# A new order for all operations of a gated recurrence with a highway layer behind it

## The chip, the cores and the metric

The kernel runs on one core of a Trainium2 chip. The metric is the time of one execution on the device, in microseconds; the lower the better. A core has five engines that work side by side, each on its own list of instructions, in order: TensorE (PE, matrix products; its weight loads are shown as PEld), VectorE (DVE), ScalarE (ACT), GpSimd (POOL) and SyncE (SP), which here issues nearly all transfers. They wait for each other by semaphores.

## The reference

There are two parts, one behind the other. For each of 4 sequences of 6336 tokens with 256 channels, a gate is made from f_logit, and a recurrence runs along the tokens:

```
sig = 1.0 / (1.0 + np.exp(-f_logit))
f = lower_bound[None, None, :] + (1.0 - lower_bound[None, None, :]) * sig
i = 1.0 - f
for t in range(S):
    h = f[:, t] * h + i[:, t] * x[:, t]
    y[:, t] = h
```

Then each token's row y goes through a highway layer:

```
H = np.maximum(y @ w_h, 0.0)
T = 1.0 / (1.0 + np.exp(-(y @ w_t + b_t)))
return T * H + (1.0 - T) * y
```

Inputs and output are float32; 25344 tokens are read twice (x and f_logit) and written once.

## The kernel before

The 25344 tokens are cut into 29 units (line 42): two of 256 tokens, three of 512, 22 of 1024, one of 512 and one of 256. The 256 channels are two halves of 128. Each unit goes through the same operations, and each operation has a letter. In a name such as f0.1 the first number is the unit and the second the half (or the piece):

- l, x: SP loads f_logit and x of the unit (line 256), tokens on the partitions.
- u: ACT makes 1 - sigmoid(f_logit), in 16 bit (line 268).
- b: the product u*x of one half (line 276), on POOL, or on DVE where the name has a v.
- i: PE transposes u of one half, 128 tokens at a time (line 284), so that channels lie on the partitions.
- f: the gate from the transposed u and the lower bound, on ACT (line 295) or, with a v, on DVE (line 293).
- p: PE transposes the products b (line 304).
- s: DVE's scan along the tokens (line 323), which is the recurrence. It begins with the last value of the unit before, of the same half, except at the start of a sequence. Its result y stands without the factor 1 - lower_bound; that factor is in the weights and in a diagonal matrix.
- z, g: PE multiplies y by the two weights (lines 335 and 115).
- t: ACT's sigmoid of z (line 348). d: DVE's max of g and y, from which y is subtracted through the weights (line 352). Line 212 takes the identity off w_h for that.
- e: the product d*t (line 358), on POOL, or on DVE with a v; a unit has one, two or three of them.
- o: PE adds y (times the diagonal, line 380) and d*t (line 381) and turns the tokens back onto the partitions. c: the copy of that into SBUF, on ACT (line 393) or, with a v, on DVE (line 391). w: SP stores it (line 397).

Operations without numbers come once: pc and pb transpose the lower bound and the bias on PE (line 194), cc makes ncc and cc of the lower bound on DVE (lines 200 and 201), cb copies the bias, dg makes the diagonal, wh and wt load the two weights, IW takes the identity off on POOL, WHa and WTa scale and shorten the weights on ACT (line 228). k*N allocates a place in PSUM and runs N matmuls on zeros (lines 126 and 115) whose results nobody reads; the three matmuls of line 154 are of that kind too.

All of this is one list, written by hand into the program as a string of names (line 49 on). The loop at line 399 goes through it, calls the function of each letter, and pins the instructions, so that each engine runs its operations in the order of the list. The number behind a colon is the slot: the buffer in SBUF, or the part of PSUM, that the result uses. An operation that reuses a slot waits until the earlier content has been read. So the list settles three things: the order on each engine, the engine of b, f, e and c, and the buffer of each result. SP's transfers are in the list too: SP issues them in order, and a store that waits for its copy holds up the loads behind it.

DVE and POOL share a port to SBUF in this program's reckoning: behind a product or scaling on DVE that the list marks, the next POOL product waits for it (line 178). Nothing makes DVE wait for POOL in the same way.

Of the kernel before, what the change touches and what calls it, by code (L numbers as in the profile page):

```python
# [19 lines left out]
def kernel(  # L20
# [37 lines left out]
b6.0:5 f6.1:2 d4.0 k*3:1 p6.1:0 s6.1:4 i6.0:1 l8:2 u7:3 z5.1:1 g5.1:2 x8:2 b7.1:6 b7.0:7 f6.0:0 t4.0 t5.1:2 i7.1:1 p6.0:0
z5.0:0 f7.1:1 d5.1:2 t5.0 o3.0:1 g5.0:2 i7.0:1 c3.0:3 s6.0:5 e5.1v w1.0 l9:3 e4.0 x9:3 w0.0 e5.2v p7.1:0 l10:4 w2.0 d5.0 e5.0
g6.0:0 z6.1:1 z6.0:2 u8:0 f7.0:3 t6.1:1 i8.0:1 e4.1v b8.0:1 b8.1:0 s7.1:6 f8.0v:2 l11:5 w3.0 t6.0 x10:4 x11:5 u9:1 d6.0:0  # L60
i8.1:0 g6.1:1 p7.0:1 s7.0:7 o5.1:2 f8.1:0 c5.1:1 o5.0:0 i9.1:0 d6.1 e6.0 p8.1:1 c5.0:0 f9.1:1 e6.2 z7.0:2 t7.0:0 o4.0:0
p8.0:0 c4.0:2 u10:2 w5.1 b9.1:3 e6.1 l12:0 w4.0 l13:1 g7.1:1 s8.1:2 i9.0:1 g7.0:2 o6.0:0 s8.0:3 i10.1:0 f9.0:3 b9.0:2 x12:0
p9.1:1 u11:3 b10.0:4 b10.1:5 b11.0:6 d7.1:2 d7.0 e7.0 z8.1:1 g8.1:2 s9.1:0 f10.1:0 p9.0:0 t8.1:2 c6.0:3 d8.1:1 i11.1:1 s9.0:1
o6.1:1 z7.1:0 f11.1:2 c6.1:1 i10.0:1 t7.1 g8.0:2 p10.0:0 z9.0:1 w6.0 w5.0 f10.0v:1 d8.0 u12:0 t9.0:1 z9.1:0 w6.1 e8.1v e7.2v
t9.1 e7.1v l14:2 x13:1 i12.1:1 f12.1:3 z8.0:2 g9.0:1 o7.1:0 s10.0:4 b11.1:7 t8.0 i11.0:1 p10.1:0 l16:3 f11.0:1 o7.0:2 u13:1
c7.0:2 d9.0:0 l15:4 e8.0 e8.2 g9.1:1 p11.0:1 s10.1:5 i13.1:0 s11.0:6 c7.1:3 f13.1:0 b12.1:0 o8.0:2 d9.1 o8.1:0 p11.1:1
i13.0:0 z10.0:1 b12.0:1 e9.0 c8.0:0 g10.0:2 s11.1:7 d10.0:2 c8.1:1 g10.1:0 f13.0:1 t10.0:0 w7.0 u14:2 w7.1 p12.1:0 z10.1:1
d10.1 z11.0:2 g11.1:0 t10.1 s12.1:2 i12.0:1 d11.1:1 t11.0:2 f12.0:2 x14:2 w8.0 w8.1 b13.1:3 z11.1:1 p12.0:0 o9.1:2 e10.0
t11.1 x15:3 l18:5 u15:3 s12.0:3 g11.0:0 p13.1:1 o9.0:1 d11.0 i14.1:0 b13.0:2 z12.0:0 c9.1:2 s13.1:0 f14.1:3 c9.0:3 o10.1:2
e11.0v x16:4 i15.1:0 p13.0:1 t12.0:1 o10.0:1 c10.1:0 f15.1:2 s13.0:1 b14.0:4 b14.1:5 c10.0:1 g12.1:0 g12.0:2 i14.0:0 w9.1  # L70
w9.0 d12.1:0 i15.0:1 d12.0 l17:0 g13.0:1 g13.1:0 z12.1:2 u16:0 f15.0:0 f14.0:1 d13.0:2 p14.0:1 b15.0:6 b15.1:7 d13.1 t12.1
w10.1 s14.0:4 w10.0 e12.0 o11.1:1 z13.0:0 u18:1 p14.1:0 o11.0:2 s14.1:5 b16.0:0 t13.0:0 x17:5 i18.0:1 l19:1 c11.1:2 w11.1
c11.0v:3 z13.1:0 f18.0:1 t13.1 g14.0:1 d14.0:1 i16.0:0 w11.0 b16.1:1 e13.0 p15.0:1 l20:2 f16.0:3 u17:2 z14.0:2 s15.0:6
o12.0:0 g14.1:1 i16.1:0 t14.0:2 b17.0:3 c12.0:0 x18:0 p15.1:1 o12.1:2 d14.1 s15.1:7 f16.1:0 w12.0 z14.1:1 c12.1:1 p16.0:0
i17.0:1 t14.1 g15.1:0 z15.0:2 w12.1 x19:1 s16.0:2 p16.1:0 f17.0:2 o13.0:1 d15.1:0 u19:3 t15.0:1 p17.0:1 o13.1:0 c13.0:2
c13.1:3 b17.1:2 e14.0 s16.1:3 z15.1:2 i17.1:0 g16.0:1 s17.0:0 g16.1:0 d16.0:2 t15.1 f17.1:3 x20:2 d16.1 u20:0 i18.1:1 z16.0:2
t16.0:0 p17.1:0 g15.0:1 z16.1:0 f18.1:0 w13.1 l21:4 b18.0:4 b18.1:5 t16.1 s17.1:1 w13.0 o14.0:2 d15.0 l22:3 i19.1:1 o14.1:0
# [12 lines left out]
e23.1 p25.0:0 c22.0:1 s25.0:0 f25.1:1 e23.2v z24.0:1 z24.1:0 g24.1:2 i26.1:0 p25.1:1 t24.0:0 f26.1:3 t24.1 d24.1:2 s25.1:1  # L90
z23.0:1 g24.0:2 w21.1 l27:3 i26.0:0 b26.0:4 b26.1:5 t23.0 o22.1:0 z25.1:1 p26.1:1 d24.0 e24.2v x27:3 u27:0 w22.0 w20.1 x28:4
g25.0:2 c22.1:3 e24.0 t25.1:1 b27.1:6 e24.1 e23.0v b27.0:7 b28.0:0 f26.0:1 s26.1:4 d25.0:0 w22.1 o23.1:0 z25.0:1 c23.1:1
p26.0:0 i27.1:1 o23.0:0 f27.1:3 t25.0 c23.0:0 g25.1:2 w21.0 s26.0:5 i27.0:1 f27.0:1 o24.1:1 p27.0:0 o24.0:0 p28.0:1 c24.1:3
# [344 lines left out]
```

## Time and profile before

| what | value |
|---|---|
| median of 3 runs | 206.66 us (206.52 to 207.08) |
| profiled execution, first to last instruction | 204.7 us |
| median of the runs less that span | 1.96 us |
| busy: DVE, ACT, PE, POOL | 193.0, 193.1, 191.6, 175.6 us |
| DMA, mean rate | 384 GB/s, 78.68 MB |

The profile gives one execution, and its span is that execution's own time from the first instruction to the last. What a run takes before and after it is in the 1.96 us. Busy time is the time in which an engine had an instruction in work; it does not say whether another engine waited for it. So the busy times are read by stretches of the span. In rows of groups, the columns are line, engine, operation, what is written and read, shape, count; then the busy time and the mean in ns; then the idle time of the engine just before, and what ended it.

### The profile page before, as it was taken

The page shows a single profiled execution, that of the slowest core. Times are in us where ns is not written, and L with a number is a line of the kernel's source. Part 1 is how long each engine was busy: PE and PEld are TensorE (multiplying, and loading weights), DVE is VectorE, ACT ScalarE, POOL GpSimd, SP SyncE. Part 2 cuts the span into 40 slices and gives each one's busy share as a digit, 9 for nine tenths or more (in the row PEclk, how much of TensorE's full clock was granted, in tenths as well). Part 3 has the DMA queues.
Part 4 walks back from the last instruction along what each step waited for, and adds up shares of the span by engine and source line. Part 5 has one row for each costly group of instructions (what it writes and reads, how often), then busy time and mean ns, then how long its engine had stood idle before and what let it go on. Part 6 is the DMA issues. An engine that isn't in the chain of part 4 may idle for free. (4 is left out here: it accounts for less than half of the span.)

```text
span 204.7 us, 4658 instructions
## 1 busy us (share of the span) xinstructions
PE 191.6 (94%) x1826; PEld 131.9 (64%) x1826; DVE 193.0 (94%) x162; ACT 193.1 (94%) x201; POOL 175.6 (86%) x98
## 2 busy tenths in 40 slices
PE   7889999989899899999999999999998999999990
PEld 2455656576567757757666577776776677677680
DVE  2799999999999999999999999999999999999990
ACT  4799999999999999999999999999999999999771
POOL 3146699899996999799999979999979999989960
PEclk9999999999999999999999999999999999999998
DMA  5999999999999999999999999999999998970986
GB/s 176 387 415 429 410 421 415 413 424 420 422 419 411 429 423 415 425 415 422 428 402 426 429 417 419 418 425 423 413 337 400 425 390 307 352 283 22 396 330 241
DMA packets 16413, 78.68 MB, mean 384 GB/s; under 512 B 1796, under 2 KB 2568, under 8 KB 10760
## 3 DMA queue, kind: packets, MB, share of 16 engines
q1 hardware_dynamic: 16384, 78.39, 94.7%
q8 instruction: 14, 0.23, 0.4%
q14 instruction: 7, 0.06, 0.1%
q10 hardware_dynamic: 8, 0.00, 0.0%
HBM read 52.43 MB, written 25.95 MB: 383 GB/s over the span
## 5 line engine op out<-in xcount | busy, mean ns | idle before, releaser
L276 POOL TENSOR_TENSOR bv<-u,x 128x1024 bf16<-128x1024 f16 (+2 forms) x53 | 104.2, 1988 | 14.8 <-DVE d L358 5.7
L323 DVE TENSOR_TENSOR_SCAN y<-f,y,bT 128x1024 bf16<-128x1024 f16 (+5 forms) x56 | 106.9, 1925 | 0.2
L358 POOL TENSOR_TENSOR d<-d,t 128x512 bf16<-128x512 bf16 (+3 forms) x32 | 70.4, 2213 | 4.1 <-DVE d L358 1.8
L352 DVE SCALAR_TENSOR_TENSOR d<-y,ncc,g 128x1024 bf16<-128x1024 bf16 (+2 forms) x58 | 63.2, 1105 | 0.3 <-PE g L115 0.2
L348 ACT ACTIVATE t<-z,bt 128x1024 bf16<-128x1024 f32 (+2 forms) x58 | 62.4, 1112 | 0.8 <-PE z L115 0.8
L295 ACT ACTIVATE f<-uT,ncc 128x1024 f16<-128x1024 f16 (+2 forms) x55 | 60.8, 1120 | 0.8 <-DVE y L323 0.2
L393 ACT COPY o<-op 128x1024 f32<-128x1024 f32 (+2 forms) x53 | 52.8, 1036 | 1.9 <-ACT t L348 1.0
L268 ACT ACTIVATE u<-l 128x2048 f16<-128x2048 f32 (+2 forms) x29 | 51.5, 1776 | 2.5 <-DMA l<-in_f_logit_dram 2.5
L380 PE MATMUL op<-diag,y 128*128 128x128 f16 x396 | 49.7, 219 | 0.9 <-ACT t L348 0.4
L381 PE MATMUL op<-ident_b,d 128*128 128x128 bf16 x396 | 49.7, 219 | 0.8 <-POOL d L358 0.8
L381 PEld LDWEIGHTS <-d 128*128 128x128 bf16 x396 | 44.0, 113 | 4.8 <-POOL d L358 1.7
L380 PEld LDWEIGHTS <-y 128*128 128x128 bf16 x396 | 44.2, 113 | 2.3
L335 PE MATMUL z<-y,w_sb 128*128 128x512 bf16 (+1 forms) x116 | 40.0, 368 | 0.8 <-DVE d L352 0.3
L335 PE MATMUL g<-y,w_sb 128*128 128x512 bf16 (+1 forms) x116 | 40.3, 368 | 0.0
L304 PE MATMUL bT<-ident_f,bv 128*128 128x128 f32 x198 | 32.1, 278 | 2.9 <-DVE y L323 1.1
L115 PE MATMUL g<-y,w_sb 128*128 128x512 bf16 x88 | 33.3, 379 | 0.0
L115 PE MATMUL z<-y,w_sb 128*128 128x512 bf16 x88 | 33.3, 379 | 0.0
L284 PE MATMUL uT<-ident_h,u 128*128 128x128 f16 x396 | 31.4, 219 | 2.0 <-DVE y L323 1.1
L284 PEld LDWEIGHTS <-u 128*128 128x128 f16 x396 | 25.9, 98 | 11.1 <-issue 3.1
L335 PEld LDWEIGHTS <-w_sb 128*128 128x128 f16 x232 | 22.3, 98 | 15.7 <-ACT f L295 0.2
L304 PEld LDWEIGHTS bT<-ident_f,bv 128*128 128x128 f32 x198 | 22.1, 140 | 13.3 <-issue 4.7
L115 PEld LDWEIGHTS <-w_sb 128*128 128x128 f16 x176 | 17.2, 98 | 15.8 <-issue 1.7
(35 smaller groups left out, 53.6 us busy)
## 6 DMA issues: line engine op xcount, KB each, us to landing
out_dram<-o SPq DMA_DIRECT2D x48, 512.0 KB, 9.7
l<-in_f_logit_dram SPq DMA_DIRECT2D x22, 1024.0 KB, 14.0
x<-in_x_dram SPq DMA_DIRECT2D x22, 1024.0 KB, 14.3
l<-in_f_logit_dram SPq DMA_DIRECT2D x4, 512.0 KB, 6.3
x<-in_x_dram SPq DMA_DIRECT2D x4, 512.0 KB, 7.6
x<-in_x_dram SPq DMA_DIRECT2D x3, 256.0 KB, 3.7
l<-in_f_logit_dram SPq DMA_DIRECT2D x3, 256.0 KB, 4.3
out_dram<-o SPq DMA_DIRECT2D x2, 256.0 KB, 14.8
```

Of the source, the lines that this page charges most:

```text
L115: return pe.add_instruction(mybir.InstMatmult(name=nc.get_next_instruction_name(), start_tensor_calc=start, stop_tensor_calc=stop, tile_si ...
L276: shared(pin(e.tensor_mul(bv[:, :nb // 2].rearrange("p k d j -> p k j d"), st[n]["u"][:, :nb, own].rearrange("p (k j) d -> p k j d", j=2), ...
L284: pin(nc.tensor.transpose(uT[:, j * P:(j + 1) * P], st[n]["u"][:, j, h * P:(h + 1) * P], ident_h))
L295: pin(nc.scalar.activation(to, of, AF.Identity, scale=ncc[:, h:h + 1], bias=1.0))
L304: pin(nc.tensor.transpose(words[:, k:k + g * (P - 1) + 1:g], pair, ident_f))
L323: pin(nc.vector.tensor_tensor_scan(y[:, c:e], st[n]["f", h][:, c:e], st[n]["bT", h][:, c:e], 0.0 if fresh else carry[h], op0=ALU.mult, op1 ...
L335: pin(nc.tensor.matmul(p[:, a:e], w, half(n, "y", ki)[:, a:e], start=ki == 0, stop=ki == NH - 1))
L348: pin(nc.scalar.activation(half(n, "t", m), st[n]["z", m][:, :tokens(n)], AF.Sigmoid, bias=bt[:, m:m + 1]))
L352: pin(nc.vector.scalar_tensor_tensor(half(n, "d", m), half(n, "y", m), ncc[:, m:m + 1], st[n]["g", m][:, :tokens(n)], op0=ALU.mult, op1=AL ...
L358: shared(pin(e.tensor_mul(st[n]["d"][:, a:c], st[n]["d"][:, a:c], st[n]["t"][:, a:c])), not eng)
L380: pin(nc.tensor.matmul(o, half(n, "y", h)[:, cols], diag[:, h], start=True, stop=False))
L381: pin(nc.tensor.matmul(o, half(n, "d", h)[:, cols], ident_b, start=False, stop=True))
```

## The change

The string is replaced by another one. The functions, the cut into units, the number of buffers and what is computed stay. The first lines of the diff show how it reads:

```
-k*3:a0 x0:0 pc:0 l0:0 l1:1 cc u0:0 k*3:1 pb:2 i0.0:1 k*4:0 dg wh u1:1 b0.1v:0 f0.0:0 b0.0v:1 i1.0:0 x1:1 l2:2 wt IW f1.0v:1 p0.0:1
...
+l0:0 k*1:a0 x0:0 u0:0 b0.0:0 i0.0:1 pc:0 cc i0.1:0 l1:1 f0.0:0 p0.0:1 f0.1v:1 x1:1 k*3:1 k*1:2 wh b0.1v:1 wt IW u1:1 s0.0:0 p0.1:0
...
```

Both hold the same 850 names, apart from the v. The new string is three lines shorter, so lines behind it have numbers that are 3 lower: DVE's gate at line 293 is line 290 there.

Operations that change engines:

| | to DVE | away from DVE |
|---|---|---|
| f (ACT or DVE) | f0.1, f1.1 (256 tokens), f2.0, f3.1 (512) | f8.0, f10.0 (1024) |
| b (POOL or DVE) | none | b0.0 (256) |
| e (POOL or DVE) | e5.0, e6.0, e24.0, e25.0 (1024 columns), e6.2, e24.1, e25.2, e27.0, e27.1 (512), e10.0, e13.0, e14.0, e20.0 (2048), e28.0, e28.1 (256) | e0.0, e0.1, e1.0, e1.1 (256), e3.1, e4.1, e5.2, e7.1, e7.2, e8.1, e23.2, e24.2 (512), e23.0 (1024), e11.0, e16.0, e19.0 (2048) |
| c (ACT or DVE) | c6.1, c8.0 (1024), c26.0 (512) | c26.1, c26.2 (512) |

The matmuls on zeros in the string go from 27 to 16. Transfers: the list of SP begins with x0 l0 l1 wh x1 l2 wt before, and with l0 x0 l1 x1 wh wt l2 now. Later l4 stands ahead of x3, l8 ahead of x7, and x19 stands behind x21, l22 and w13.0.

At three places the order of an engine is shown, before and now. The first is DVE's beginning; 128x256 is a half of unit 0 or 1, and y<-f,bT is the scan. Before:

```order
L200 TENSOR_SCALAR ncc<-lbT 128x2
L201 TENSOR_SCALAR cc<-lbT 128x2
L217 TENSOR_SCALAR diag<-ident_h,cc 128x128 x2
L276 TENSOR_TENSOR bv<-u,x 128x2x128 x2
L293 TENSOR_SCALAR f<-uT,ncc 128x256
L207 COPY bt<-tbT 128x2
L323 SCALAR_TENSOR_TENSOR y<-f,bT 128x256
L276 TENSOR_TENSOR bv<-u,x 128x2x128 x2
```

And now:

```order
L197 TENSOR_SCALAR ncc<-lbT 128x2
L198 TENSOR_SCALAR cc<-lbT 128x2
L290 TENSOR_SCALAR f<-uT,ncc 128x256
L273 TENSOR_TENSOR bv<-u,x 128x2x128
L320 SCALAR_TENSOR_TENSOR y<-f,bT 128x256
L273 TENSOR_TENSOR bv<-u,x 128x2x128
L214 TENSOR_SCALAR diag<-ident_h,cc 128x128 x2
L320 SCALAR_TENSOR_TENSOR y<-f,bT 128x256
L290 TENSOR_SCALAR f<-uT,ncc 128x256
```

The first gate and the first scan stand further ahead, one product b has gone to POOL, and the diagonal comes behind the first scan.

The second place is PE's beginning, where lbT is what DVE's ncc is made of. Before:

```order
L115 LDWEIGHTS zeros
L115 MATMUL idle<-zeros 128x512
L194 MATMUL lbT<-ident_f,lb 128x2
L126 LDWEIGHTS zeros
L126 MATMUL idle<-zeros 128x512
L115 LDWEIGHTS zeros
L115 MATMUL idle<-zeros 128x512
L115 LDWEIGHTS zeros
L115 MATMUL idle<-zeros 128x512
L194 MATMUL tbT<-ident_f,tb 128x2
L284 LDWEIGHTS u
L284 MATMUL uT<-ident_h,u 128x128
```

And now:

```order
L123 MATMUL idle<-zeros 128x512
L281 LDWEIGHTS u
L281 MATMUL uT<-ident_h,u 128x128
L281 LDWEIGHTS u
L281 MATMUL uT<-ident_h,u 128x128
L191 MATMUL lbT<-ident_f,lb 128x2
L281 LDWEIGHTS u
L281 MATMUL uT<-ident_h,u 128x128
```

The lower bound's transpose has gone behind the first two transposes of u0, and the matmuls on zeros ahead of it are four where there were six.

The third place is DVE's end, with the units 26 to 28. Before:

```order
L352 SCALAR_TENSOR_TENSOR d<-y,ncc,g 128x512
L391 COPY o<-op 128x512
L352 SCALAR_TENSOR_TENSOR d<-y,ncc,g 128x256
L391 COPY o<-op 128x512
L352 SCALAR_TENSOR_TENSOR d<-y,ncc,g 128x256
L391 COPY o<-op 128x512
```

And now:

```order
L355 TENSOR_TENSOR d<-d,t 128x512
L388 COPY o<-op 128x512
L349 SCALAR_TENSOR_TENSOR d<-y,ncc,g 128x256
L388 COPY o<-op 128x512
L349 SCALAR_TENSOR_TENSOR d<-y,ncc,g 128x256
L355 TENSOR_TENSOR d<-d,t 128x256 x2
```

The two products of unit 28, which POOL made, stand at DVE's end, behind the last d; the third copy is ACT's.

More of the change, by code (lines that the diff above doesn't have):

```diff
@@ L58 @@
[L58 to L77, printed above, removed]
@@ new lines @@
+z5.1:0 e4.1 s6.0:4 e4.0 i7.0:1 d5.1:2 p6.1:0 b7.1:6 t5.1:2 s6.1:5 z5.0:1 f7.0:1 i7.1:1 g5.0:0 u8:0 o3.0:2 f7.1:3 d5.0 p7.1:0 s7.1:6
+b7.0:7 i8.0:1 b8.0:1 t5.0 g6.0:0 z6.0:1 f8.0:2 c3.0:3 w0.0 w2.0 u9:1 p7.0:1 d6.0:0 x9:3 i8.1:0 l10:4 s7.0:7 e5.2 z6.1:2 g6.1:0 t6.1:0
+o4.0:2 f8.1:0 b8.1:0 t6.0 c4.0:4 d6.1 i9.1:1 p8.0:0 e5.0v z7.1:0 z7.0:1 l12:5 g7.0:2 e6.2v e5.1v f9.1:3 i9.0:1 e6.0v s8.0:0 d7.0:1
+t7.1:1 g7.1:0 u10:2 t7.0 e6.1 f9.0:1 p8.1:0 o6.0:2 d7.1 c6.0:0 o6.1:1 i10.0:1 o5.0:0 l11:0 w1.0 b9.1:2 s8.1:1 f10.0:2 b9.0:3 x10:4
@@ new lines @@
+c5.0:2 g8.0:2 c6.1v:1 x11:5 i10.1:0 u11:3 p9.1:1 g8.1:1 e7.2 d8.0:0 e7.0 b10.0:4 z8.0:0 s9.1:4 f10.1:0 z8.1:2 p9.0:0 d8.1 w4.0 i11.1:1
+b10.1:5 w3.0 x12:0 l13:1 t8.0:2 s9.0:5 w6.0 w6.1 b11.1:6 t8.1 f11.1:3 o7.1:0 o5.1:1 l15:2 k*0:2 p10.1:1 c7.1:4 u12:0 z9.1:2 x13:1
+b11.0:7 g9.1:0 t9.1:0 s10.1:2 p10.0:0 c5.1:3 i12.0:1 z9.0:2 d9.1:2 f12.0:1 s10.0:3 e7.1 g9.0:0 w5.0 i11.0:1 o7.0:1 d9.0 t9.0 p11.0:0
+l14:3 z10.1:2 f11.0:0 u13:1 p11.1:1 g10.1:0 e8.2 e8.0 b12.0:1 e8.1 x14:2 c7.0:0 t10.1:1 s11.0:6 s11.1:7 i13.1:0 o8.1:1 o8.0:2 i12.1:1
@@ L99 @@
+o27.1:0 z28.1:a0 c27.0:3 w26.1 z28.0:a1 d28.1:1 g28.0:1 c27.1v w26.0 t28.1:1 d28.0 e28.1v w27.0 t28.0 e28.0v o28.0:2 c28.0:1 o28.1:a0
+c28.1:4 w28.0 w28.1
 """
```

63 lines of the change are left out of this document (35 added, 28 removed).

## The prediction

> **What bounds the kernel now.** I read the page first (span, busy time, slices), then the busy time by stretch, then the groups by shape, then the order of time at both ends. The page:
>
> ```profile
> span 204.7 us, 4658 instructions
> PE 191.6 (94%) x1826; PEld 131.9 (64%) x1826; DVE 193.0 (94%) x162; ACT 193.1 (94%) x201; POOL 175.6 (86%) x98
> DVE  2799999999999999999999999999999999999990
> ACT  4799999999999999999999999999999999999771
> ```
>
> Four engines stand at 86 to 94%, so the average tells nothing. The slices do: DVE is short of full only in the first two slices and the last. By stretch (length; busy time of PE, its weight loads, DVE, ACT and POOL, each with its count of instructions; granted clock; share of the DMA engines; GB/s):
>
> ```profile
> 20.00:180.00 160.00, 154.56 (x1507) 108.58 (x1508) 159.68 (x113) 160.00 (x150) 150.12 (x66) 1.00 1.01 409
> 180.00:190.00 10.00, 10.00 (x106) 7.49 (x106) 9.83 (x9) 8.91 (x10) 9.53 (x8) 1.00 0.39 155
> 190.00:200.00 10.00, 9.69 (x115) 7.40 (x113) 9.13 (x14) 8.00 (x14) 7.69 (x7) 1.00 0.92 361
> ```
>
> For 160 us DVE is idle for 0.32 us and ACT for none; POOL has 9.9 us to spare. DVE stays at 91 to 98% to the end, while ACT falls to 80%. The DMA engines are full too, but the waits (total, times, longest) show what the transfers cost the engines:
>
> ```profile
> ACT u L268 <- DMA l<-in_f_logit_dram: 2.5, 2, 1.3
> POOL bv L276 <- DMA x<-in_x_dram: 0.2, 1, 0.2
> ```
>
> That is 2.7 us in all, and the 2.5 fall on the first two loads. So the bound is DVE's own work, with ACT close behind; a charge on late transfers mends something that hardly costs here. The question is what the new table does to DVE's work and to the little time DVE is idle.
>
> **DVE's work.** The table also hands operations to other engines. Rows by shape (count, then busy and mean ns):
>
> ```profile
> L358 DVE TENSOR_TENSOR d<-d,t 128x2048 bf16<-128x2048 bf16 x4 | 5.3, 1354 | 0.0
> L358 DVE TENSOR_TENSOR d<-d,t 128x512 bf16<-128x512 bf16 x13 | 5.1, 424 | 0.1
> L358 DVE TENSOR_TENSOR d<-d,t 128x256 bf16<-128x256 bf16 x4 | 0.9, 282 | 0.0
> L358 DVE TENSOR_TENSOR d<-d,t 128x1024 bf16<-128x1024 bf16 x1 | 0.7, 678 | 0.0
> L293 DVE TENSOR_SCALAR f<-uT,ncc 128x1024 f16<-128x1024 f16 x2 | 2.5, 1258 | 0.0
> L293 DVE TENSOR_SCALAR f<-uT,ncc 128x256 f16<-128x256 f16 x1 | 0.5, 483 | 1.4 <-PE uT L284 1.4
> L391 DVE COPY o<-op 128x1024 f32<-128x1024 f32 x1 | 1.2, 1199 | 0.0
> L391 DVE COPY o<-op 128x512 f32<-128x512 f32 x3 | 2.1, 691 | 0.4 <-PE op L381 0.2
> L276 DVE TENSOR_TENSOR bv<-u,x 128x256 bf16<-128x256 f16 x4 | 1.5, 434 | 0.0
> L323 DVE TENSOR_TENSOR_SCAN y<-f,y,bT 128x256 bf16<-128x256 f16 x4 | 2.7, 720 | 0.0
> ```
>
> The tables give the counts (the last row, a scan, is for the head). Gained: f of 256, two (0.97); f of 512, two; product d·t of 1024, three (2.03), of 2048, one (1.35); copy of 1024, two (2.40). No row has f of 512 on DVE: each lies between 0.48 and 1.26, and the straight line between those rows gives 0.74, so 1.48 for two. Sum 8.23. Lost: f of 1024, two (2.52); d·t of 512, three (1.27), of 256, two (0.56); b of 256, one (0.43); copy of 512, one (0.69). Sum 5.47. Net +2.76, and +2.24 to +3.80 by the ends of f. Two corrections. Neighbours overlap a little:
>
> ```profile
> 98.43 1.20 DVE L391 COPY o<-op 128x1024 f32<-128x1024 f32 x1
> 99.54 1.27 DVE L352 SCALAR_TENSOR_TENSOR d<-y,ncc,g 128x1024 bf16<-128x1024 bf16 x1
> ```
>
> The copy's 1.20 would end at 99.63, and the next begins at 99.54; with one instruction more in all that is -0.1. And the mean of 1354 ns holds one product that was held up (below); a free one takes 1.20: -0.15. I take **+2.5**. The scans and the 58 d stay as they are.
>
> ACT goes the other way:
>
> ```profile
> L295 ACT ACTIVATE f<-uT,ncc 128x1024 f16<-128x1024 f16 x42 | 53.0, 1278 | 0.0
> L295 ACT ACTIVATE f<-uT,ncc 128x512 f16<-128x512 f16 x8 | 5.4, 687 | 0.8 <-DVE y L323 0.2 <-PE uT L284 0.2
> L295 ACT ACTIVATE f<-uT,ncc 128x256 f16<-128x256 f16 x5 | 2.4, 491 | 0.0
> L393 ACT COPY o<-op 128x1024 f32<-128x1024 f32 x42 | 47.1, 1163 | 0.0
> L393 ACT COPY o<-op 128x512 f32<-128x512 f32 x9 | 5.1, 588 | 1.8 <-ACT t L348 1.0 <-PE op L381 0.8
> ```
>
> Two f of 1024 more (2.56) and one copy of 512 (0.59), less two f of 512 (1.37), two of 256 (0.98) and two copies of 1024 (2.33): **-1.5**. POOL is lighter by more, PE by 11 dummy matmuls. In 20 to 180 us these cannot be paid to DVE: it has 0.32 us to win there. Nothing covers the +2.5.
>
> **The head.** In order of time:
>
> ```profile
> 2.87 1.06 PE L115 MATMUL idle<-zeros 128*128 128x512 bf16 x2
> 4.14 0.63 ACT L268 ACTIVATE u<-l 128x512 f16<-128x512 f32 x1 [1.29 <-DMA l<-in_f_logit_dram]
> 4.16 0.16 DVE L200 TENSOR_SCALAR ncc<-lbT 128x2 f32<-128x2 f32 x1 [3.03 <-PE lbT L194]
> 5.74 0.81 PE L115 MATMUL idle<-zeros 128*128 128x512 bf16 x3
> 5.96 0.63 ACT L268 ACTIVATE u<-l 128x512 f16<-128x512 f32 x1 [1.19 <-DMA l<-in_f_logit_dram]
> 6.73 0.87 POOL L212 TENSOR_TENSOR w_raw<-w_raw,ident_f 128x128 f32<-128x128 f32 x2 [4.48 <-DMA w_raw<-in_moe_w_h_dram]
> 9.80 0.90 ACT L228 ACTIVATE w_sb<-w_raw,cc 128x256 f16<-128x256 f32 x2
> 10.81 0.84 DVE L352 SCALAR_TENSOR_TENSOR d<-y,ncc,g 128x256 bf16<-128x256 bf16 x2
> ```
>
> l0 moves up one place, worth 0.64 (256 KB at the 409 GB/s of the middle), so u0 runs 3.5 to 4.1. l1 stays third, so the second wait, to 5.96, stays. lbT, from which ncc comes, now stands behind u0's first transposes on PE: ncc at about 4.6, 0.45 later than now. Then, by the rows above, f0.1 (0.48), b0.1 (0.43) and the first scan (0.72) run to 6.3; x1 takes wh's old fourth place and arrives near 6.7; b1.0, diag, the second scan, f1.1, b1.1, f1.0 and two scans end at 10.4. The first d needs g0.1, which on PE now stands behind z0.1 and so behind the second scaled weight (WTa) on ACT, about 10.0; d starts at 11.05 against 10.81, with 0.5 us more of DVE's work done. That is **0.2 to 0.3 saved**. The other end: the seven dummies that now stand between the first bT and the transposes of u1 cost 0.53 each at the early rate (1.06 for two) or 0.27 at the later (0.81 for three). At the early rate f1.1 comes a good 1 us later, and the head loses **0.8**. I take 0.0, nearer to the warm row, since it falls at 5.74, before most of these dummies.
>
> The Trainium skill ("TensorE: Matmul & The Clock Gate", Part 1: The HAM clock gate) says that the array starts throttled and is released by about 3.4 us of sustained activity. By that rule this change loses: its PE has only four dummies up to about 2.9 us and then waits for u0, so the release would come a window later and the head would cost the 0.8. The trace agrees that the rate doubles (1.06 for two, then 0.81 for three), though its granted clock reads full from the first slice; what a thinner start does no row shows.
>
> **The tail.** DVE is idle for about 0.6 us between 180 us and its end at 199.54 (0.17, and 0.87 less the last 0.46):
>
> ```profile
> 198.13 0.48 DVE L352 SCALAR_TENSOR_TENSOR d<-y,ncc,g 128x256 bf16<-128x256 bf16 x1
> 198.85 0.69 DVE L391 COPY o<-op 128x512 f32<-128x512 f32 x1 [0.24 <-PE op L381]
> 198.95 0.67 POOL L358 TENSOR_TENSOR d<-d,t 128x256 bf16<-128x256 bf16 x1 [0.41 <-ACT t L348]
> ```
>
> Now the end hangs on the last d, done at 198.61: POOL's product behind it ends at 199.62, 1.0 later, and DVE's last copy is off that path. In the change the copies stand ahead of the last d (+0.69 before it), both last products are DVE's (0.28 each, 0.56 less before it), and from that d to their end is about 0.5 instead of 1.0. Together -0.4 against the ledger, which had the end at DVE's last instruction. What follows (matmuls, copies, stores) is unchanged. Of the 0.6 idle I credit 0.1: value **-0.5**, ends -1.0 and +0.5.
>
> **The middle.** 0.32 us idle, and one product held up:
>
> ```profile
> 143.39 6.41 POOL L276 TENSOR_TENSOR bv<-u,x 128x1024 bf16<-128x1024 f16 x3
> 149.09 1.78 DVE L358 TENSOR_TENSOR d<-d,t 128x2048 bf16<-128x2048 bf16 x1
> 85.81 1.20 DVE L358 TENSOR_TENSOR d<-d,t 128x2048 bf16<-128x2048 bf16 x1
> ```
>
> POOL's product ends at 149.80; DVE's was issued at 149.09 and ends 1.07 after that, so it waited some 0.6 for POOL. I take **-0.5** of these 0.9, since ACT, PE and POOL are all lighter; ends -0.9 and, with new hold-ups, +2.2.
>
> **Sum.** 204.7 + 2.5 + 0.0 - 0.5 - 0.5 = 206.2 for the span. The median of the runs lies 1.96 above the profiled span (206.66 - 204.7), which I keep: **208.2 us**, 0.7% slower.
>
> **Rivals.**
>
> *Holes swallow it.* From ncc at 4.16 to its end DVE has 195.4 us, of which 192.7 busy (193.0 less 0.3 for the memset before): 2.7 idle, and 0.6 of hold-up. If of these 3.3 only 0.9 in the head came back: 4.6 + 195.4 - 3.3 + 2.5 + 0.9 = 200.1, and 5.2 behind it: 205.3, a run of 207.2, which is no change. For: every other engine is lighter. Against: it needs a middle and a tail without a hole, which the present order, as dense, does not have.
>
> *ACT binds, not DVE* (the other sign). ACT shows 160.00 of 160.00 busy, DVE 159.68. If DVE's rows only stretch to ACT's pace, -1.5 on ACT sets the time: 203.2, a run of 205.1. It decides where DVE's instructions would be shorter when fed sooner. Against: a DVE that waited for ACT would show it as idle time, and it shows 0.32 in 160; and ACT is at 80% at the end.
>
> *More hold-ups.* DVE's products of 1024 or wider go from 5 to 9. One that starts while POOL is in a product waits for half of it on average, 1.1 of 2.14 (6.41 for three). Two such hits more: 206.2 + 2.2 = 208.4, a run of 210.4. Against: one in 27 waits now, and the total of DVE's two-tensor products falls to 25. The Trainium skill ("SBUF — State Buffer", SBUF: two separate sides) says that such a pair shares one port as an exclusive lock and the later one blocks; the 1.78 against 1.20 agrees.
>
> *A load comes late.* x3 now stands behind l4, x7 behind l8 and x19 far back. One place of 1 MB at 409 GB/s is 2.6 us. It decides where the products wait for x longer than POOL has spare (9.9 in 160), and DVE's scan of that unit then waits too; with half of it passed on: 206.2 + 1.3, a run of 209.5.
>
> **How the numbers follow.** About 0.3% (0.6 us) is what a measurement of this kernel can tell from no change. Forecast 0.50, hold-ups 0.10, late load 0.05: slower 0.65. Holes 0.20: the same. ACT 0.15: faster. The range reaches down into the no-change case and up to just short of the hold-ups: 205.9 to 209.9. The forecast's own range, with the ends of f (-0.5, +1.0), head (-0.3, +0.8) and tail (-0.5, +1.0) added in squares, is 207.4 to 209.8.
>
> **What would show it.** Right: DVE's busy time near 195.5 at 159.5 or more of 160 in the middle, ACT near 191.5, u0 near 3.5 and ncc near 4.6 us. Wrong: DVE idle for some us in the middle (then waits bind, and the row before the hole names which), the bT dummies at 0.5 us past 7 us (the head lost), DVE products of 2048 over 1.3 us (hold-ups), or a span under 205.3, which would mean that the ledger or the floor is false.

## The result and the profile after

The changed kernel takes 209.44 us (median of 4 runs, 208.42 to 209.68) where the kernel before takes 206.76 beside it (206.52 to 207.08): a ratio of 1.012, with an interval of 1.010 to 1.015. It is slower by 2.7 us, or 1.2%. The prediction said 208.2, with a range of 205.9 to 209.9. Now and then an execution is some per cent longer at a lower granted clock; the ratios leave such ones out.

The profiled execution is the quickest of the four, 208.42 with a span of 206.6; the other three have spans of 207.5 to 207.9. That spread turns out to matter. In all 121 runs on record with a span of their own, of both kernels and their variants, the time less that span is 1.74 to 1.86. So the 1.96 that stands ahead of the prediction set the median of three runs against the span of a faster one; it isn't what a run takes around its span. First the page of the changed kernel:

```profile
span 206.6 us, 4580 instructions
PE 189.2 (92%) x1789; PEld 131.2 (63%) x1815; DVE 195.3 (95%) x163; ACT 192.9 (93%) x198; POOL 168.9 (82%) x100
DVE  1799999899999999999999999999999999999991
ACT  4589999999999999999999999999999999999881
```

DVE's busy time is 2.3 us up on 193.0. ACT's is almost the same (192.9 after 193.1), though three operations were taken from it on balance. By stretch:

```profile
20.00:180.00 160.00, 152.22 (x1469) 107.27 (x1492) 159.24 (x110) 158.89 (x150) 146.54 (x69) 1.00 1.00 406
180.00:190.00 10.00, 9.95 (x98) 6.96 (x97) 10.00 (x9) 9.58 (x10) 8.27 (x8) 1.00 0.60 220
190.00:200.00 10.00, 9.95 (x119) 7.83 (x119) 9.90 (x15) 8.75 (x14) 4.40 (x4) 1.00 0.72 283
```

From 20 to 180 us DVE has now 0.76 us idle (0.32 before), and from 180 to 200 only 0.1. To see where the 1.9 us between the two spans lie, I cut both executions at the first d, at 180 us and at the end of DVE's last instruction. The columns are as before: length, then busy time of PE, its weight loads, DVE, ACT and POOL. The kernel before:

```profile
0.00:10.81 10.81, 9.05 (x41) 3.74 (x42) 5.31 (x16) 6.63 (x12) 2.49 (x13) 1.00 0.79 289
10.81:180.00 169.19, 162.72 (x1571) 113.30 (x1568) 168.73 (x128) 168.88 (x165) 155.87 (x71) 1.00 1.01 410
180.00:199.54 19.54, 19.37 (x214) 14.61 (x213) 18.96 (x22) 16.56 (x23) 17.14 (x14) 1.00 0.64 254
199.54:204.70 5.16, 0.45 (x5) 0.28 (x5) 0.00 (x1) 0.98 (x3) 0.08 (x1) 0.83 0.64 246
```

And the changed kernel:

```profile
0.00:11.91 11.91, 8.97 (x38) 4.01 (x39) 6.01 (x16) 5.98 (x11) 3.15 (x14) 1.00 0.78 285
11.91:180.00 168.09, 158.59 (x1519) 111.09 (x1543) 167.33 (x121) 166.47 (x160) 153.03 (x76) 1.00 1.00 407
180.00:202.08 22.08, 21.11 (x228) 15.72 (x227) 21.95 (x28) 19.75 (x26) 12.67 (x11) 1.00 0.70 266
202.08:206.60 4.52, 0.56 (x7) 0.39 (x7) 0.00 (x1) 0.74 (x2) 0.00 (x0) 0.95 0.59 222
```

DVE's idle time up to the first d goes from 5.50 to 5.90 (+0.40); from there to 180 us from 0.46 to 0.76 (+0.30); from 180 us to its end from 0.58 to 0.13 (-0.45). What follows DVE's end goes from 5.16 to 4.52 (-0.64), and DVE's work is +2.29. The sum is +1.90, the difference of the spans (work is DVE's busy time). This is an account, not yet a cause: it says where the time is, and not what would move it.

The head in order of time. DVE, ACT and PE of the changed kernel:

```profile
3.48 0.63 ACT L265 ACTIVATE u<-l 128x512 f16<-128x512 f32 x1 [0.64 <-DMA l<-in_f_logit_dram]
4.79 0.16 DVE L197 TENSOR_SCALAR ncc<-lbT 128x2 f32<-128x2 f32 x1 [3.66 <-PE lbT L191]
6.27 1.06 PE L112 MATMUL idle<-zeros 128*128 128x512 bf16 x2
7.12 0.63 PE L123 MATMUL idle<-zeros 128*128 128x512 bf16 x1
8.17 0.60 PE L112 MATMUL idle<-zeros 128*128 128x512 bf16 x2
8.01 0.69 DVE L320 TENSOR_TENSOR_SCAN y<-f,bT 128x256 bf16<-128x256 f16 x1 [0.59 <-PE bT L301]
9.14 0.48 DVE L290 TENSOR_SCALAR f<-uT,ncc 128x256 f16<-128x256 f16 x1 [0.44 <-PE uT L281]
11.91 0.45 DVE L349 SCALAR_TENSOR_TENSOR d<-y,ncc,g 128x256 bf16<-128x256 bf16 x1
```

u0 comes at 3.48 as said, so l0 in front did save its 0.66. But then PE is late: at 6.27 two zeros still take 1.06, and only at 8.17 do two take 0.60. Before, the same rows stood at 2.87 and 5.74. DVE waits for PE's bT (0.59) and uT (0.44), and the first d comes at 11.91 instead of 10.81. The changed kernel was run and profiled a second time: 209.38 us (208.96 to 209.74, 5 runs), ratio 1.0156 (1.0137 to 1.0176). It was expected that a profiled execution above 208.4 has its first d later than 11.9; this one took 209.62, and it has. The low rate goes further there:

```profile
6.51 1.06 PE L112 MATMUL idle<-zeros 128*128 128x512 bf16 x2
8.43 1.06 PE L112 MATMUL idle<-zeros 128*128 128x512 bf16 x2
11.27 0.59 PE L112 MATMUL idle<-zeros 128*128 128x512 bf16 x2
13.08 0.46 DVE L349 SCALAR_TENSOR_TENSOR d<-y,ncc,g 128x256 bf16<-128x256 bf16 x1
```

There the low rate holds to about 10 us, the first d comes at 13.08, and the span is 207.8. Both executions take the same time from the first d to the end: 206.6 - 11.91 = 194.7 and 207.8 - 13.08 = 194.7. So the difference between these two executions is made in the head.

### The profile page after: what moved, and what is told of

It reads as the page before. It is cut to its first block, busy times and chain, and to the rows that moved or that the text cites. A ratio compares the mean times of both kernels' runs of the same rounds, so it can differ in the third digit from the quotient of the medians.

```text
span 206.6 us, 4580 instructions
## 1 busy us (share of the span) xinstructions
PE 189.2 (92%) x1789; PEld 131.2 (63%) x1815; DVE 195.3 (95%) x163; ACT 192.9 (93%) x198; POOL 168.9 (82%) x100
## 4 chain that ended last, share of the span: by engine, by line
PE 51%; ACT 18%; DVE 16%; issue 9%; POOL 3%; DMA 1%; ACTq 0%; DVEq 0%; POOLq 0%
DVE y L320 10%; PE g L332 7%; PE uT L281 7%; PE op L377 7%; PE bT L301 6%; PE op L378 6%; PE z L332 6%; ACT f L292 5%; ACT o L390 5%; PE z L112 5%; PE g L112 5%; DVE d L349 4%; ACT u L265 4%; ACT t L345 3%; POOL bv L273 3%
## 5 line engine op out<-in xcount | busy, mean ns | idle before, releaser
L355 POOL TENSOR_TENSOR d<-d,t 128x512 bf16<-128x512 bf16 (+3 forms) x33 | 64.3, 1963 | 10.7 <-DVE d L349 5.9
L345 ACT ACTIVATE t<-z,bt 128x1024 bf16<-128x1024 f32 (+2 forms) x58 | 58.8, 1044 | 1.1 <-PE z L332 0.6
L292 ACT ACTIVATE f<-uT,ncc 128x1024 f16<-128x1024 f16 (+2 forms) x53 | 57.4, 1093 | 2.4 <-PE uT L281 1.3
L390 ACT COPY o<-op 128x1024 f32<-128x1024 f32 (+2 forms) x52 | 48.4, 972 | 2.5 <-PE op L378 0.9
L265 ACT ACTIVATE u<-l 128x2048 f16<-128x2048 f32 (+2 forms) x29 | 49.8, 1722 | 0.9 <-DMA l<-in_f_logit_dram 0.9
L377 PE MATMUL op<-diag,y 128*128 128x128 f16 x396 | 49.1, 219 | 1.4 <-DVE d L349 0.4
L378 PE MATMUL op<-ident_b,d 128*128 128x128 bf16 x396 | 49.0, 219 | 0.9 <-DVE d L355 0.9
L332 PE MATMUL z<-y,w_sb 128*128 128x512 bf16 (+1 forms) x112 | 39.0, 367 | 1.0 <-DVE y L320 0.4
L112 PE MATMUL g<-y,w_sb 128*128 128x512 bf16 x79 | 29.9, 379 | 0.1
L112 PE MATMUL z<-y,w_sb 128*128 128x512 bf16 x77 | 29.2, 379 | 0.1
```

What stands on the lines that cost most here:

```text
L112: return pe.add_instruction(mybir.InstMatmult(name=nc.get_next_instruction_name(), start_tensor_calc=start, stop_tensor_calc=stop, tile_si ...
L292: pin(nc.scalar.activation(to, of, AF.Identity, scale=ncc[:, h:h + 1], bias=1.0))
L332: pin(nc.tensor.matmul(p[:, a:e], w, half(n, "y", ki)[:, a:e], start=ki == 0, stop=ki == NH - 1))
L345: pin(nc.scalar.activation(half(n, "t", m), st[n]["z", m][:, :tokens(n)], AF.Sigmoid, bias=bt[:, m:m + 1]))
L355: shared(pin(e.tensor_mul(st[n]["d"][:, a:c], st[n]["d"][:, a:c], st[n]["t"][:, a:c])), not eng)
L377: pin(nc.tensor.matmul(o, half(n, "y", h)[:, cols], diag[:, h], start=True, stop=False))
```

## The experiments

Each time has its median, range and number of runs, and its ratio to the kernel before on the same chip. Since the head varies, kernels are also compared by the time from the first d to the end of the span. It is one execution each, and it separates head and rest only where PE's rate has doubled before the first d. That time for the profiled executions, without those of the next two kernels:

| kernel | span | first d | from there to the end |
|---|---|---|---|
| before | 204.7 | 10.81 | 193.9 |
| changed | 206.6 | 11.91 | 194.7 |
| changed, again | 207.8 | 13.08 | 194.7 |
| changed, four zeros at the start | 207.7 | 12.97 | 194.7 |
| changed, no gap on PE | 205.4 | 10.63 | 194.8 |
| changed, no zeros ahead of u1 | 207.1 | 11.81 | 195.3 |
| changed, two copies on ACT | 209.6 | 13.07 | 196.5 |
| changed, without two products | 207.9 | 13.01 | 194.9 |
| changed, without t | 206.7 | 12.49 | 194.2 |
| changed, without both | 206.7 | 13.02 | 193.7 |
| before, two d twice | 206.9 | 10.88 | 196.0 |
| before, two t twice | 207.1 | 11.33 | 195.8 |

### The order alone, and the engines alone

The first pair took the change apart: the new order with the old engines for b, f, e and c, and the old order with the new engines. In the string only the v of the names differs, for instance:

```
-l0:0 k*1:a0 x0:0 u0:0 b0.0:0 i0.0:1 pc:0 cc i0.1:0 l1:1 f0.0:0 p0.0:1 f0.1v:1 ...
+l0:0 k*1:a0 x0:0 u0:0 b0.0v:0 i0.0:1 pc:0 cc i0.1:0 l1:1 f0.0:0 p0.0:1 f0.1:1 ...
```

> The new order, with b, f, e and c on the engines that they had before. Theory (DVE's work sets the time): DVE's work falls back by 2.5 us, its busy time to about 193, and the time from 209.4 to about 207, with up to 1 us more where a product now meets POOL at a bad moment. Rival (the order and its waits cost the time, not the engines): the time stays at 209 or above with DVE idle for some us in the middle.

> The old order, with b, f, e and c on the engines of the change. Theory (DVE's work): DVE busy about 195.5, and 206.7 + 2.5 = 209.2, up to 211 if wide products meet POOL products. Rival (the order costs the time): 206.7 to 207.3.

Measured: 238.48 us (237.51 to 253.63, 6 runs), ratio 1.153 (1.149 to 1.157), and 233.89 us (231.37 to 237.72, 6 runs), ratio 1.128 (1.123 to 1.133). Both missed by far. The profiled execution of the first ran at a granted clock of 0.76, and its durations aren't compared. The second's ran at 0.97, with a span of 233.2. Three waits of DVE in it, and two instructions:

```profile
DVE d L352 <- PE g L115: 5.2, 4, 3.3
DVE y L323 <- PE bT L304: 4.6, 5, 2.2
DVE d L352 <- PE g L335: 2.9, 3, 1.2
134.74 4.07 POOL L358 TENSOR_TENSOR d<-d,t 128x2048 bf16<-128x2048 bf16 x1 [4.93 <-ACT t L348]
135.65 4.25 DVE L358 TENSOR_TENSOR d<-d,t 128x2048 bf16<-128x2048 bf16 x1
```

Of the 28.5 us that the span grew, DVE is idle for 16.7, mostly waiting for PE (total, times and longest wait above). The other 11.8 are busy time, though the ledger is only +2.5. Of these some 7 are hold-ups of the kind that the prediction feared: the DVE product above ends 1.09 us behind POOL's and takes 4.25, another took 5.17, and the mean of the five products of 2048 is 2.61 us, where the changed kernel has 1.21. The pair told nothing on the ledger: at 27 to 32 us it is a cost of another kind. What follows is that order and engines are one decision here. With buffers handed on in a fixed order and engines without slack, a product that lands on another engine arrives at another time, and what stands behind it waits. Which of the moved operations starts this, the pair doesn't tell.

### Is DVE full, and is ACT?

Instead of moving work, the next kernels add some and leave order and engines as they are. In the kernel before, two d of 1024 (units 12 and 18) are made twice, the second time over the first. In a sister kernel, two t of 1024 on ACT are made twice.

```
-        pin(nc.vector.scalar_tensor_tensor(half(n, "d", m), ...
+        for _ in range(2 if (n, m) in ((12, 0), (18, 0)) else 1):
+            pin(nc.vector.scalar_tensor_tensor(half(n, "d", m), ...
```

> The kernel before, with two d of 1024 (units 12 and 18, first half) made twice on DVE; the second writes the same values. Theory (DVE is full): 2 x 1.17 = 2.3 us more, 209.1. Rival (ACT sets the time and DVE has slack that its rows hide): 206.7 to 207.3.

Measured: 208.75 us (208.59 to 209.36, 6 runs) beside 206.78, ratio 1.0106 (1.0075 to 1.0137): +2.0 for 2.3 added. From the first d to the end it is 196.0 after 193.9, +2.1.

> The kernel before, with two t of 1024 (units 12 and 18, first half) made twice on ACT, 2 x 1.0 us; the second writes the same values. Theory (DVE alone sets the time, ACT has some slack between its starts): 0 to 0.8 more, 206.8 to 207.6. Rival (ACT is bound as tightly as DVE): 2.0 more, 208.8.

Measured: 208.83 us (208.49 to 209.01, 4 runs) beside 206.25, ratio 1.0129 (1.0111 to 1.0146): +2.6 for 2.0 added, of which 0.5 is a later first d in the profiled execution; from there it is 195.8 after 193.9, +1.9. So in the kernel before, at these places, ACT is as tight as DVE, and the prediction's "ACT close behind" was too weak. The stretch in which one of the doubled operations lies, in the kernel before with t twice:

```profile
100.00:140.00 40.00, 37.33 (x368) 26.76 (x372) 38.68 (x26) 39.97 (x38) 37.56 (x16) 1.00 1.02 421
```

DVE, which had 39.88 of these 40 us, has 38.68, while ACT stays full: DVE idles for 1.3 us behind an engine that has got more to do.

### Two copies from DVE to ACT in the changed kernel

If DVE set the pace alone, taking two copies of 1024 off it should help.

```
-c5.0:2 g8.0:2 c6.1v:1 x11:5 ...
+c5.0:2 g8.0:2 c6.1:1 x11:5 ...
-f13.1:2 d10.1:1 c8.1:1 c8.0v:2 ...
+f13.1:2 d10.1:1 c8.1:1 c8.0:2 ...
```

> The change with the copies c6.1 and c8.0 (1024 each) on ACT again, as before the change. Theory (DVE's work sets the time): DVE loses 2 x 1.13 us and ACT gains 2 x 0.9, of which its 1.1 us of idle time in the middle takes a part: 1.0 to 2.2 less, 207.2 to 208.4. Rival (ACT is as full as DVE there and only changes places with it, or the waits of the order decide): 209.2 or more.

Measured: 210.59 us (210.25 to 211.38, 5 runs), ratio 1.0221 (1.020 to 1.0241), where the changed kernel beside it had 209.38, ratio 1.0156 (1.0137 to 1.0176). It is 1.2 slower, which is the rival's side. The stretch in which the second of the two copies lies, first in the changed kernel, then in this one:

```profile
60.00:100.00 40.00, 38.00 (x384) 27.14 (x388) 40.00 (x26) 40.00 (x38) 38.17 (x18) 1.00 1.02 419
60.00:100.00 40.00, 36.79 (x366) 26.18 (x369) 37.23 (x23) 40.00 (x38) 36.58 (x18) 1.00 1.01 417
```

Both engines were full, and now DVE is idle for 2.8. From the first d to the end it is 196.5 after 194.7: +1.8, and two copies from start to start are 1.8 on ACT (0.89 each). So in the changed kernel, too, ACT has no room here.

### Relief of DVE, of ACT, and of both in the changed kernel

The sharper question is what the changed kernel gains from having less to do. The first kernel leaves out the products d*t of units 13 and 14 on DVE (2.26 us); the second also the four t of these units on ACT (4.0 us); the third leaves out only the t, and its products take d in place of t. The strings differ only in the names left out, and the third kernel has in the function of e:

```
+        by = "d" if n in (13, 14) else "t"
-        shared(pin(e.tensor_mul(st[n]["d"][:, a:c], st[n]["d"][:, a:c], st[n]["t"][:, a:c])), not eng)
+        shared(pin(e.tensor_mul(st[n]["d"][:, a:c], st[n]["d"][:, a:c], st[n][by][:, a:c])), not eng)
```

> The changed kernel without the two products d*t of units 13 and 14 (2048 columns each, on DVE, 1.13 each by its rows): the output of these two units lacks the factor t. DVE has 2.26 us less to do in the middle; ACT, PE and POOL keep their work. Theory (DVE's own work sets the pace): 2.0 to 2.3 faster than the changed kernel, 207.0 to 207.4 where that one has 209.3. Rival (ACT is as full and sets the pace as much, as the two copies moved to ACT suggested): under 0.7 faster, 208.6 or more, with DVE idle for another 1.5 to 2 us in the middle.

> As the kernel without the two products, and also without the four sigmoids t of units 13 and 14 (ACT, four of 1024, about 1.0 each by the other kernel's repeated ones): the output of these units lacks the factor t. DVE has 2.26, ACT 4 us less to do, POOL and PE the same. Theory (DVE sets the pace alone): no faster than without the two products alone. Rival (DVE and ACT set it together): 1 to 2 faster than that run, so that both together give the 2.0 to 2.3 that the products alone did not.

> The changed kernel without the four sigmoids t of units 13 and 14 (ACT, four of 1024, 1.00 each from start to start by its own trace); the two products on DVE stay and take d in place of t, so that the output of these two units is another. ACT has 4.0 us less to do in the middle; DVE, PE and POOL keep their work. Measured from the first d to the end of the span, the changed kernel took 194.7, without the two products 194.9, without both 193.7. Theory (ACT alone is the bound at this place): 193.4 to 193.9, as without both, and a time near 208.1. Rival (both are equally full, and relief of one leaves the other): 194.4 to 194.9 and a time of 209 or more.

Measured: without the products 209.38 us (208.99 to 209.65, 4 runs), ratio 1.0139 (1.0118 to 1.0161), no faster than the changed kernel. Without products and t 208.14 (207.34 to 208.51, 6 runs), ratio 1.0082 (1.0063 to 1.0102). Without t 208.47 (207.91 to 208.91, 6 runs), ratio 1.0079 (1.0058 to 1.0099). By the time from the first d, against 194.7: +0.2 with DVE relieved, -0.5 with ACT relieved, -1.0 with both. The forecast for the third run fits neither theory: 194.2 lies between the two ranges. By the medians alone the third run is as quick as the second (ratios 1.0079 and 1.0082); their heads differ, with the first d at 12.49 and 13.02 in the profiled executions.

The stretch from 100 to 140 us, in which most of these operations lie. The changed kernel:

```profile
100.00:140.00 40.00, 38.99 (x364) 27.23 (x369) 39.95 (x27) 39.85 (x38) 34.49 (x15) 1.00 1.02 422
```

Without the two products:

```profile
100.00:140.00 40.00, 38.98 (x367) 27.06 (x372) 37.86 (x25) 39.86 (x38) 34.42 (x15) 1.00 1.02 418
```

Without t alone:

```profile
100.00:140.00 40.00, 38.41 (x369) 27.27 (x373) 39.98 (x28) 37.47 (x35) 34.82 (x15) 1.00 1.02 422
```

Without both:

```profile
100.00:140.00 40.00, 38.87 (x373) 27.57 (x378) 38.34 (x26) 37.93 (x36) 35.25 (x15) 1.00 1.02 422
```

Relieve DVE, and it idles for 2.1 us while ACT stays full. Relieve ACT, and it idles for 2.5 while DVE stays full. The holes in DVE that the first kernel gets name ACT:

```profile
110.27 2.35 DVE L320 TENSOR_TENSOR_SCAN y<-f,y,bT 128x1024 bf16<-128x1024 f16 x1 [1.02 <-ACT u L265]
119.63 2.35 DVE L320 TENSOR_TENSOR_SCAN y<-f,y,bT 128x1024 bf16<-128x1024 f16 x1 [0.94 <-ACT f L292]
```

So at this place ACT is a little ahead of DVE and both are full: DVE's 2.26 us less had no price there, ACT's 4.0 less gave 0.5. Even with both relieved only 1.0 of DVE's 2.26 comes back, and DVE and ACT idle for 1.7 and 2.1 in the stretch. Of the four longer holes there, two name PE (bT, 0.94, and z, 0.96) and two ACT (0.60 and 0.94). What is behind PE then (its own 38.87 of 40, or the transfers at a share of 1.02) no run here tells apart.

### The head

Three kernels change nothing but the matmuls on zeros. The first puts four in place of one at the start:

```
-l0:0 k*1:a0 x0:0 u0:0 ...
+l0:0 k*4:a0 x0:0 u0:0 ...
```

> The change with four matmuls on zeros instead of one in its first place, so that PE is busy until u0 is there. Theory (the thin start keeps PE at its low rate until about 8 us): the low rate ends near 5 us, the first d comes at 11.1 instead of 11.9, and the time falls by 0.5 to 0.8, to about 208.7. Rival (the head's loss is taken up later, or the clock doesn't hang on this): 209.4, within 0.2.

Measured: 208.70 us (207.05 to 209.85, 12 runs) beside 206.78, ratio 1.0082 (1.0052 to 1.0111). The forecast of 208.7 came out, but not by its mechanism, so it is luck: in the profiled execution the low rate ended near 10 us instead of 5, and the first d came at 12.97 instead of 11.1. The spread is the finding: spans of 205.3 to 208.0. If 194.7 behind the first d holds for all of them, the first d lies anywhere from 10.6 to 13.3. (The kernel before, beside it, has spans of 203.9 to 205.8 in 17 runs, so the head need not be all of the spread.)

The second takes away the seven zeros that stand between the first bT and the transposes of u1 in the new order.

```
-... x1:1 k*3:1 k*1:2 wh ...
+... x1:1 k*0:1 k*0:2 wh ...
-b1.0v:2 WHa k*3:a1 i1.1:1 ...
+b1.0v:2 WHa k*0:a1 i1.1:1 ...
```

> The change without the seven matmuls on zeros between the first bT and the transposes of u1. Theory (at the low rate these seven cost 3 us on the path of f1.1): f1.1 starts near 7.5 instead of 9.1, the first d comes at 11.1 to 11.3, bound by the scaled weights, and the time falls by 0.6 to 0.8 to 208.7. Rival (they keep PE's rate up and are worth their place): PE's rate doubles later than 8.2 us and the time stays or rises, 209.4 to 210.4.

Measured: 208.81 us (208.55 to 208.93, 4 runs), ratio 1.0128 (1.0111 to 1.0145), 0.6 quicker than the changed kernel beside it and with a narrower range (0.4 instead of 0.8). The zeros cost their time. Without them PE keeps the low rate to about 12 us in the profiled execution, the latest of all profiles here, and the first d has a new wait:

```profile
10.29 0.63 PE L332 MATMUL g<-y,w_sb 128*128 128x256 bf16 x2
11.57 0.63 PE L332 MATMUL z<-y,w_sb 128*128 128x256 bf16 x2
12.37 0.38 PE L332 MATMUL z<-y,w_sb 128*128 128x256 bf16 x2
11.81 0.48 DVE L349 SCALAR_TENSOR_TENSOR d<-y,ncc,g 128x256 bf16<-128x256 bf16 x1 [0.53 <-PE g L332]
```

The real matmuls g and z take 0.63 where the last row of PE takes 0.38. So part of this head's loss lies behind the first d, and its 195.3 in the table is no measure of the rest. The forecast was 11.1 to 11.3 for the first d and 208.7 for the time; the time came out, the first d (11.81) did not. The third kernel goes the other way: four zeros at the start, and two more behind the transposes of u0, so that PE has no gap above some tenths until 6 us.

```
-l0:0 k*1:a0 x0:0 u0:0 b0.0:0 i0.0:1 pc:0 cc i0.1:0 l1:1 ...
+l0:0 k*4:a0 x0:0 u0:0 b0.0:0 i0.0:1 pc:0 cc i0.1:0 k*2:2 l1:1 ...
```

> The changed kernel with three more matmuls on zeros at the start and two more between the last transpose of u0 and the first transpose of its products, so that PE has no gap of more than some tenths from 1.2 to about 6 us. In the changed kernel's own profiled executions the rate of PE doubled at about 8 and about 10 us, and with it the first d came at 11.91 and 13.08. Theory (PE's rate doubles after a stretch without a gap): the doubling comes by 7 us in every execution, the seven zeros ahead of u1's transposes cost 0.27 each instead of 0.53, the first d comes at 11.0 to 11.6, the time is 207.9 to 208.3 and the spread under 0.5 us. Rival (the moment of doubling has to do with something else than PE's own gaps): the dummies at 0.53 until 8 us or later, first d at 12 or later, 208.5 to 209.5 with the same spread of 1 us.

Measured: 207.64 us (207.14 to 208.21, 6 runs) beside 206.40, ratio 1.0064 (1.0045 to 1.0084). PE and DVE in its head:

```profile
4.50 0.22 PE L191 MATMUL lbT<-ident_f,lb 2*128 2x2 f32 x1
4.77 0.38 PE L123 MATMUL idle<-zeros 128*128 128x512 bf16 x1
6.89 0.59 PE L112 MATMUL idle<-zeros 128*128 128x512 bf16 x2
10.63 0.46 DVE L349 SCALAR_TENSOR_TENSOR d<-y,ncc,g 128x256 bf16<-128x256 bf16 x1
```

The rate has doubled by 4.5, the first d comes at 10.63, before that of the old kernel, and the time is 1.7 under the changed kernel's 209.38. The first d came 0.4 sooner than its range, the time 0.3 sooner, and the spread is 1.1 and not under 0.5. The profile itself doesn't test the theory: the rate doubled ahead of the two added zeros (4.77), on a list that up to there is that of the kernel with four zeros, whose rate doubled near 10. Two other comparisons bear on it. All fourteen profiles on record sort by PE's gaps. In the five in which PE has no gap of over 0.1 us until the doubling (this kernel and four with the old order), it comes at 4.5 to about 7 us; in the nine with a gap of 0.5 us or more before 5.5 us (all of the new order), at about 8 to about 12. The latest of the five, the old order with t twice:

```profile
6.25 1.22 PE L115 MATMUL idle<-zeros 128*128 128x512 bf16 x3
```

Three zeros take 1.22 there, between the 1.49 of three at the low rate and the 0.81 at the high one. And the 12 runs with four zeros fall in two groups: five spans of 205.3 to 206.0, as in this kernel (205.4 to 206.4, 6 runs), and seven of 206.7 to 208.0. That fits a rate that doubles either ahead of the gap at 5.1 us or much later. So the theory stands in its main part, by comparison of profiles and not by a run that changes the gap alone, and how long a start without a gap takes still varies by over 2 us.

This is the best version of the new order that was run, and it is still 1.2 us slower than the kernel before (ratio 1.0064). None was found that beats it.

## Why the prediction was right, and where it was not

**The sum.** Forecast for the span 206.2, measured 206.6 in the profiled execution, with what lies around it at 1.82 where I kept 1.96 (it is 1.74 to 1.86 in every run, so this term was some 0.15 too high). By its terms:

| term | forecast | profiled execution |
|---|---|---|
| ledger of DVE's work | +2.5 (2.24 to 3.80) | +2.9 |
| head | 0.0 (-0.3 to +0.8) | +0.4; +1.5 in the second profile |
| middle | -0.5 (-0.9 to +2.2) | -0.3 |
| tail | -0.5 (-1.0 to +0.5) | -1.1 |
| sum | +1.5 | +1.9 |

DVE's busy time rose by 2.29 net of the 0.6 of hold-up that is gone, so the ledger came to 2.9. The two bounds that I had to estimate held, in the groups by shape of the changed kernel:

```profile
L290 DVE TENSOR_SCALAR f<-uT,ncc 128x512 f16<-128x512 f16 x2 | 1.5, 734 | 0.0
L355 DVE TENSOR_TENSOR d<-d,t 128x2048 bf16<-128x2048 bf16 x5 | 6.0, 1214 | 0.0
```

f of 512 takes 734 ns (straight line: 740), and the five wide products take 1214 ns each: no hold-up, so that rival is out. The middle lost the hold-up and gained 0.30 of idle time, mostly one hole at 39.45 where a scan waits 0.59 for PE. The tail gave twice what I credited: its idle time was filled by 0.45, not 0.1, and the end came 0.64 sooner behind DVE's last instruction, not 0.4. No load came late: POOL and DVE wait for no x anywhere in the trace, so that rival is out too.

**The step that failed is the head**, "I take 0.0, nearer to the warm row, since it falls at 5.74, before most of these dummies". That row belongs to the old order, whose PE had six zeros up to 3.9 us; I carried it over to one that has four and then waits for u0. The low rate lasted to about 8 us in the profiled execution and to about 10 in the second. The head thus costs +0.4 and +1.5 (the first d later by 1.10 and 2.27, less 0.70 and 0.81 us more of work done by then), and the three other spans of 207.5 to 207.9 would put the first d at 12.8 to 13.2, if the rest is 194.7 in them too. By the prediction's own sign, zeros at 0.5 us past 7 us, the head was lost. The upper end of +0.8, which I gave to the low rate, was too small as well: the median of the runs lies 1.2 us above 208.2, and a head as in the second profile accounts for that. The run without a gap on PE shows it from the other side: the first d at 10.63, the remainder at 194.8 unchanged.

The Trainium skill ("TensorE: Matmul & The Clock Gate", Part 1: The HAM clock gate) was on the right side of this: by its rule the thin start loses a window. The gapless start doubled 3.3 us after PE's first matmul (1.19 to 4.50), which agrees with its about 3.4; the old order's starts without a gap took up to nearly 6. It also says that the window runs free of the kernel's start and the moment so differs from run to run; the trace agrees, more widely than the 0.5 us that the page gives, as the last section shows.

**"Nothing covers the +2.5"** came out as an account, but its reason was incomplete. I read 159.68 of 160 us on DVE as the bound and ACT's 160.00 as second. The doubled t in the kernel before cost as much as the doubled d; in the changed kernel DVE's 2.26 us less gave nothing at all, and its 159.24 of 160 us missed the sign of 159.5. Two engines, each full and each waiting for the other's products, set the time together at the places tried. So the ledger of DVE alone is no price list, and that its sum fitted is partly luck: from the first d on, the new order loses 0.8 us, and whether DVE's added work or ACT's place in the new order makes them is not settled by these runs. The forecast that ACT's busy time falls to 191.5 failed (192.9). It was added up from rows that hold more than ACT's work. Two neighbours each of the kernel before and of the changed one:

```profile
102.47 1.46 ACT L348 ACTIVATE t<-z,bt 128x1024 bf16<-128x1024 f32 x1
103.47 1.37 ACT L393 COPY o<-op 128x1024 f32<-128x1024 f32 x1
103.74 1.25 ACT L345 ACTIVATE t<-z,bt 128x1024 bf16<-128x1024 f32 x1
104.74 1.16 ACT L390 COPY o<-op 128x1024 f32<-128x1024 f32 x1
```

The same t is recorded with 1.46 and with 1.25 us, yet in both the next operation starts 1.00 behind it. A hole shorter than this overhang doesn't show as idle time. From start to start (1.00 and 0.57 for f of 1024 and 512, 0.36 for 256; copies 0.89 and 0.47, the closest in the traces) the moves give -1.2. But between 20 and 180 us ACT's starts lie 3.9 us further apart in all than the closest of their kind, 1.8 before, of which the idle time shows only 1.1 and 0.0. So ACT has less work and more holes, most of them hidden in its busy time.

**The rivals.** *Holes swallow it* is excluded by the interval of the ratio. *ACT binds, not DVE* had half of the mechanism: ACT does bind, beside DVE. Its conclusion, that ACT's lighter ledger then makes the kernel faster, was wrong: ACT's work fell by about 1.2, but ACT lost more than that in holes, and DVE was full as well.

## What to carry to other kernels

Where two engines are full and feed each other, price a change by adding to or taking from each of them in turn and then from both; a busy share of 99.8% on one does not make its ledger the time. An order and the engines that it was made for are one thing: swapping either alone cost 27 to 32 us, many times the 2.7 that both together cost. And where the first real work hangs on TensorE, try to keep it busy without a gap from its first matmul: five matmuls on zeros were worth 1.7 us here, and no move of work that was tried gained anything.

## What was not expected of the hardware

The moment at which TensorE's rate doubles is not settled by the program alone. The kernel with four zeros at the start and the one without a gap run the same list on PE up to 4.7 us. In the latter the rate had doubled by 4.50 (the rows above: 0.22 for lbT). In the former's profiled execution, at the same place and still at 8.30:

```profile
4.50 0.26 PE L191 MATMUL lbT<-ident_f,lb 2*128 2x2 f32 x1
8.30 1.06 PE L112 MATMUL idle<-zeros 128*128 128x512 bf16 x2
```

The only gap in between is 0.59 us, ahead of 5.68, and it can't have to do with what was different at 4.50. The two executions ran on different chips; but the runs of the first kernel, all on one chip, fall in the two groups named above. So the rate of an engine that is busy from 1.19 us on had doubled at 4.5 in one execution and, behind a gap of 0.59 us, not before 10 in another, and the spans of one kernel differ by up to 2.7 us (205.3 to 208.0). The granted clock reads 1.00 in every stretch of the head in both profiles; only the spacing of the zeros shows the rate.
